# Preparing one batch entry instead of two before the first token blocks of a Fourier mixing and SoLU kernel

## The chip, the cores and the metric

The kernel runs on one core of a Trainium2 chip. A core has a matrix engine (PE in the profile, with its weight loads as PEld), a vector engine (DVE), an activation engine (ACT), a general engine (POOL), a queue engine that only issues transfers (SP), and 16 DMA engines that carry the transfers which SP, ACT and POOL issue. Every engine works through its own instructions in order. The metric is the time of one execution in device microseconds.

## What is computed

```python
def _attn_ref(x, filt_r, filt_i):            # x (8, 3136, 256), filters (1569, 256)
    X = np.fft.rfft(x, axis=1)
    Y = X * (filt_r + 1j * filt_i)[None, :, :]
    return np.fft.irfft(Y, n=x.shape[1], axis=1).astype(np.float32)

def _moe_ref(x, w_in, w_out, g_ln):          # x (25088, 256), w_in (256, 1024), w_out (1024, 256)
    h = x @ w_in
    e = np.exp(h - np.max(h, axis=-1, keepdims=True))
    solu = h * (e / (np.sum(e, axis=-1, keepdims=True) + 1e-09))
    mu = np.mean(solu, axis=-1, keepdims=True)
    var = np.mean((solu - mu) ** 2, axis=-1, keepdims=True)
    return ((solu - mu) / np.sqrt(var + 1e-06) * g_ln) @ w_out
```

The second function takes the output of the first, its eight batch entries laid end to end. The inputs of the second part are in 64-bit floats and are converted on the chip.

## The kernel before

**The Fourier part** splits the length 3136 as 49 x 64 and is done for each batch entry in three stages with two trips through DRAM. Stage one (`first`, L213) works in eight pieces per entry: a piece `x` of 98 partitions is loaded, multiplied with the table `wf_t` (tile `pa`), copied by ACT to `t1` and stored to `d1`. Stage two (the spectrum) works in units: a unit loads `t2` from `d1` (`fetch`), multiplies it with the table `de` (`forward`, tile `pb`), multiplies the result with the complex filter `f` on DVE (`multiply`: products `pr`, `pi` and a term `pt` for each, part 0 for the real, part 1 for the imaginary part), multiplies back (`inverse`, tile `pc`), copies it to `g` and stores it to `d2`. A spectrum of two entries at once ("paired") has 13 units of one pair of rows of the table each, a spectrum of one entry 7 units of two pairs. Stage three (`back`, L305) loads a piece `t4` from `d2` (`fetch_back`, L297), multiplies it with `wi_t` (tile `py`) and ACT copies it into `y`.

**The buffer `y`** holds two entries: 256 channels as two chunks of 128 partitions, 2 x 3136 tokens. Even entries stand in its first half, odd entries in its second.

**The token part** works on 196 blocks of 128 tokens, one per step `k` (`step`, L750). Pairs of blocks share seven products instead of eight in both matrix multiplications, so POOL forms sums of `y` (`pair_sums`) and of the turned activations (`project_sums`). A step issues the products `m` with `w_in` (L541), the exponential (L573), the normalization (L589), a 32x32 transpose `turn` on DVE (L599), four transfers that regroup it into `solu_t` (L611), and, nine steps later (`LAG`), the products `o` with `w_out` (L653). After the last block nine steps drain the pipeline.

**What sets the order.** The opening, up to `y` of entry 0, is laid out by a scheduler from the order in the code. There the entries 0 and 1 go through stages one and two together (group 0), and entry 0 through stage three; entry 1's stage three is spread over steps 0 to 19. From the first block on the order is written out by hand: the lists `first_of`, `early`, `mid`, `late`, `stores`, `products` and `loads` hold for each step the jobs of the Fourier part that go at a given place of the step. `GROUPS` gives for each group of entries the first step and the number of steps over which its pieces and its units are spread:

```python
    ((0, 1), None, None),
    ((2,), (0, 6), (9, 14)),
    ((3, 4), (6, 13), (23, 26)),
```

A unit at step t is fetched at the end of step t - 2, goes forward in step t (`early`), has part 0 at the end of step t (`late`), part 1 at the start of step t + 1 (`products`), goes back at the end of step t + 1 and is stored in step t + 2. Loads of `x` and of `t4` share three buffers (`r`), and each is issued up to three steps ahead, not before the load three before it is used:

```python
        at = max(t - 3, row_loads[n - 3][0] if n >= 3 else -1)
```

In the blocks POOL issues the loads of `x` and `f` and the stores of `d1` and `d2`, ACT the loads of `t2` and `de`, SP the loads of `t4`, the regrouping and the output. In the opening ten matmuls on nothing that is needed (`idle`, L422) run on PE between stage two and stage three. The filters stay in SBUF during the opening; for the later spectra they are copied from the inputs to `f_dram` by eight transfers in steps 0 to 3. The weights are converted from 64 bits by DVE in eight blocks of ten instructions (`load_float64`): four of `w_in`, then `weight_sums`, and four of `w_out`.

Of the kernel before, what the change touches and what calls it, by code (L numbers as in the profile page):

```python
# [10 lines left out]
FP32 = mybir.dt.float32  # L11
# [19 lines left out]
NG = 5  # L31
# [9 lines left out]
    ((0, 1), None, None),  # L41
    ((2,), (0, 6), (9, 14)),
    ((3, 4), (6, 13), (23, 26)),
    ((5, 6), (32, 28), (64, 29)),
    ((7,), (94, 18), (116, 24)),
]
EPS_LN, EPS_SM = 1e-6, 1e-9
# [41 lines left out]
def kernel(  # L89
# [30 lines left out]
    nc.sync.dma_start(out=wf_t, in_=wf_dram)  # L120
# [43 lines left out]
    def by_16(dmas, out, in_, engines=16):  # L164

        n = out.shape[0] // engines * engines
        dmas[0](out=out[:n], in_=in_[:n])
        dmas[1](out=out[n:], in_=in_[n:])

    class Spectrum:  # L170
# [6 lines left out]
        def __init__(self, n, pools, load, load_de):  # L177
            self.n, self.entries, self.pools = n, GROUPS[n][0], pools
            self.load, self.load_de = load, load_de
            self.paired = len(self.entries) == 2  # L180
# [23 lines left out]
        def fetch_x(self, i, dmas, split):  # L204
            b, ch = divmod(i, NH // NCH)
            self.xs[i] = xt = self.pools["r"].tile([P, NCH, C], FP32, name=f"x_{self.n}_{i}", tag="r")
            xb = x[self.entries[b]]
            for h, first, step in ((0, NCH * ch, C), (1, N2 - 1 - NCH * ch, -C)):
                split(dmas, xt[N1 * h:N1 * h + N1],
                      bass.AP(tensor=xb.tensor, offset=xb.offset + first * C,  # L210
                              ap=[[N2 * C, N1], [step, NCH], [1, C]]))
# [16 lines left out]

        def fetch(self, i, dma):
            self.t2s[i] = self.pools["t2"].tile([P, 4, C], FP32, name=f"t2_{self.n}_{i}", tag="t2")  # L230
# [3 lines left out]
        def fetch_de(self, i):  # L234
            self.des[i] = self.load_de(*self.units[i])

        def fetch_filter(self, i):
            self.fs[i] = self.load(*self.units[i])
# [17 lines left out]
        def multiply(self, i, part, add):  # L256
# [5 lines left out]
            def fk(k):  # L262
# [3 lines left out]
            out, term = (self.pools["p"].tile([P, 2, C], FP32, name=f"p{tag}_{self.n}_{i}", tag=tag)[  # L266
                rows, 0:w, :] for tag in ("ri"[part], "t"))
# [8 lines left out]
        def inverse(self, i, pss):  # L276
# [6 lines left out]
            self.gs[i] = self.pools["g"].tile([P, 4, C], FP32, name=f"g_{self.n}_{i}", tag="g")  # L283
# [34 lines left out]
    with ExitStack() as st:  # L318
        pools = {name: pool(name + "0", bufs, stack=st)
                 for name, bufs in (("r", 6), ("t1", 4), ("t2", 3), ("p", 2), ("g", 2))}  # L320
        fpool = pool("fp", 1, stack=st)
        wpool = pool("wp", 2, stack=st)
# [34 lines left out]
        def load_tables(g):  # L357
            i0, n = NG * g, min(NG, NP - NG * g)
            tables[g] = fpool.tile([P, NG, 2, 2, NQ], FP32, name=f"de_{g}", tag=f"de{g}")
            nc.gpsimd.dma_start(out=tables[g][:, 0:n],  # L360
                                in_=de_dram[i0:i0 + n].rearrange("i p k u q -> p i (k u q)"))
            filters[g] = f = fpool.tile([P, NG, 2, C], FP32, name=f"f_{g}", tag=f"f{g}")
            for place, k, held, rows in all_filter_rows(i0, n):
                nc.gpsimd.dma_start(out=f[place, 0:held, k, :], in_=rows)

# [11 lines left out]
        def resident(i, pairs):  # L377
            return filters[i // NG][:, i % NG:i % NG + pairs]

        sp = Spectrum(0, pools, resident, lambda i, pairs: tables[i // NG][:, i % NG:i % NG + pairs])  # L380
# [5 lines left out]
        for i in range(2 * NH // NCH):  # L386
            sp.fetch_x(i, (nc.sync.dma_start, nc.sync.dma_start), partial(by_16, engines=15))
            sp.first(i, (0, 1), ps_h.tile([P, 2, 512], FP32, name=f"pa_0_{i}", tag="h"),
                     nc.scalar.copy)
            sp.store_first(i, 0, lambda out, in_: by_16((nc.scalar.dma_start, nc.gpsimd.dma_start), out, in_))  # L390
# [478 lines left out]
```

## Time and profile before

| | us |
|---|---|
| median of three runs | 1861.56 |
| lowest and highest run | 1852.31, 1864.58 |
| the profiled execution | 1860.94 |
| its span (first to last instruction) | 1859.2 |
| PE busy | 1676.2 |
| DVE busy | 1229.4 |
| POOL busy | 1071.6 |
| ACT busy | 948.0 |
| mean granted clock of PE, share of full | 0.945 |

The profile counts an engine as busy while one of its instructions runs; issuing a transfer does not count. The span is cut into stretches below, each with the engines' busy time, the clock granted to PE and what the DMA engines moved. A row of a wait reads "who <- for whom: total us, times, longest". Where an engine waits for several things, the row names the last.

### The profile page before, as it was taken

To read this page: it belongs to the slowest core of one execution; us is meant where nothing else is said; L and a number is where in the kernel's file an instruction comes from. 1 tells how busy PE (TensorE), PEld (TensorE's weight loads), DVE (VectorE), ACT (ScalarE), POOL (GpSimd) and SP (SyncE) were. 2 spreads that over 40 slices of the span, in tenths; PEclk is the share of its full clock that TensorE was granted. 3 is DMA by queue.
4 is the path that set the end of the run, shared out by engine and by line. 5 is a ranking of instruction groups with operands and counts; after the bars stand their busy time and mean duration, and the time that the engine had idled before them with its cause. 6 is when DMAs were issued, how large, how long until landed. Compare 5 with 4: busy or idle time off the path is not lost.

```text
span 1859.2 us, 29143 instructions
## 1 busy us (share of the span) xinstructions
PE 1676.2 (90%) x9192; PEld 1106.6 (60%) x9192; DVE 1229.4 (66%) x2583; ACT 948.0 (51%) x1715; POOL 1071.6 (58%) x1281
## 2 busy tenths in 40 slices
PE   4547978879999999999999999998999999999996
PEld 1111733546556666675665666776676777777776
DVE  0585045456877777567778776667777776778773
ACT  1111345435455555565555556664555666665562
POOL 4134255555656776555654566655556666666664
PEclk8677588889999999999999999999999999999999
DMA  8754457776668776556556565655656454444443
GB/s 231 215 180 154 117 175 195 198 200 176 170 177 219 208 204 175 143 142 177 164 154 171 157 144 147 163 132 145 173 163 154 109 124 125 111 109 103 104 109 101
DMA packets 356249, 293.69 MB, mean 158 GB/s; under 512 B 63105, under 2 KB 324290, under 8 KB 356096
## 3 DMA queue, kind: packets, MB, share of 16 engines
q1 hardware_dynamic: 292960, 167.96, 35.9%
q0 software_dynamic: 33824, 91.09, 16.2%
q10 hardware_dynamic: 29312, 32.78, 5.9%
q8 instruction: 75, 1.23, 0.3%
q14 instruction: 78, 0.64, 0.1%
HBM read 110.68 MB, written 81.50 MB: 103 GB/s over the span
## 4 chain that ended last, share of the span: by engine, by line
PE 62%; DVE 15%; DMA 11%; issue 4%; POOL 3%; ACT 3%; SPq 1%; ACTq 0%; DVEq 0%; POOLq 0%
PE o L653 25%; PE m L541 23%; PE py L311 6%; PE pa L219 4%; DMA solu_t<-turn 3%; DVE h L589 3%; DMA x<-in_x_dram 3%; DMA t<-d 2%; PE pc L244 2%; PE pb L244 2%; DVE turn L599 2%; DVE pr L271 1%; DVE pt L270 1%; DMA raw<-in_moe_w_out_dram 1%; DVE h L565 1%
## 5 line engine op out<-in xcount | busy, mean ns | idle before, releaser
L653 PE MATMUL o<-w_out_sb,solu_t 128*128 128x128 f32 x3136 | 406.9, 279 | 22.2 <-DVE ot L672 20.2
L653 PEld LDWEIGHTS o<-w_out_sb,solu_t 128*128 128x128 f32 x3136 | 383.2, 194 | 60.6 <-issue 32.9
L541 PE MATMUL m<-w_in_sb,s 128*128 128x512 f32 x784 | 406.7, 612 | 3.9 <-ACT h L551 3.8
L591 ACT ACTIVATE e<-h,nmu 128x1024 f32<-128x1024 f32 x196 | 225.3, 1150 | 358.8 <-DVE h L589 356.4
L653 PEld LDWEIGHTS o<-w_out_sb,u 128*128 128x128 f32 x2352 | 310.3, 193 | 147.7 <-issue 118.6
L541 PE MATMUL m<-w_in_sb,y 128*128 128x512 f32 x588 | 307.1, 606 | 17.4 <-DVE nmax L565 13.9
L653 PE MATMUL o<-w_out_sb,u 128*128 128x128 f32 x2352 | 315.2, 278 | 7.6 <-ACT ot L665 7.5
L519 POOL TENSOR_TENSOR u<-solu_t 128x512 f32<-128x512 f32 x98 | 149.8, 1528 | 282.2 <-DMA solu_t<-turn 176.2
L589 DVE SCALAR_TENSOR_TENSOR h<-e,rsum,h 128x1024 f32<-128x1024 f32 x196 | 283.5, 1446 | 7.4 <-DVE rsum L586 0.6
L672 DVE SCALAR_TENSOR_TENSOR ot<-o,rs_t,ot 128x128 f32<-128x128 f32 x294 | 101.6, 345 | 265.2 <-ACT ot L665 226.3
L565 DVE CUSTOM_DVE_ANT_0 h<-m,h 128x512 f32<-128x512 f32 x196 | 134.5, 686 | 212.8 <-ACT h L551 132.7
L551 ACT COPY h<-m 128x512 f32<-128x512 f32 x294 | 172.6, 587 | 155.6 <-PE m L541 102.4
L519 POOL TENSOR_TENSOR u<-solu_t,u 128x512 f32<-128x512 f32 x98 | 141.4, 1443 | 181.7 <-PE o L653 180.8
L599 DVE STREAM_TRANSPOSE turn<-h 128x1024 f32<-128x1024 f32 x196 | 242.5, 1237 | 1.5
L573 ACT ACTIVATE e<-h,nmax 128x1024 f32<-128x1024 f32 x196 | 224.7, 1147 | 0.0
L219 PE MATMUL pa<-x,wf_t 98*100 98x512 f32 x256 | 150.1, 700 | 65.6 <-DMA x<-in_x_dram 54.1
L311 PEld LDWEIGHTS py<-wi_t,t 100*128 100x128 f32 x1024 | 142.4, 212 | 72.6 <-issue 51.5
L541 PEld LDWEIGHTS m<-w_in_sb,s 128*128 128x128 f32 x784 | 131.1, 195 | 90.0 <-issue 78.8
L311 PE MATMUL py<-wi_t,t 100*128 100x98 f32 x1024 | 148.1, 297 | 18.0 <-DMA t<-d 15.1
L314 ACT COPY y<-py 128x392 f32<-128x392 f32 x128 | 107.4, 839 | 91.2 <-PE py L311 89.9
L519 POOL TENSOR_TENSOR solu_t<-solu_t,solu_t 128x512 f32<-128x512 f32 x98 | 145.9, 1489 | 7.7
L541 PEld LDWEIGHTS m<-w_in_sb,y 128*128 128x128 f32 x588 | 98.0, 192 | 86.5 <-issue 50.1
(75 smaller groups left out, 1866.6 us busy)
## 6 DMA issues: line engine op xcount, KB each, us to landing
solu_t<-turn SPq DMA_DIRECT2D x784, 128.0 KB
out_dram<-ot SPq DMA_DIRECT2D x196, 128.0 KB
t<-d SPq DMA_DIRECT2D x56, 400.0 KB
d<-g POOLq DMA_DIRECT2D x75, 256.0 KB, 4.2
d<-t POOLq DMA_DIRECT2D x96, 200.0 KB, 4.3
x<-in_x_dram POOLq DMA_DIRECT2D x96, 196.0 KB, 6.0
t<-d ACTq DMA_DIRECT2D x50, 256.0 KB
t<-d SPq DMA_DIRECT2D x25, 256.0 KB
```

Source lines behind the costliest of these rows:

```text
L219: nc.tensor.matmul(out=ps[0:NK, j], lhsT=wf_t, rhs=self.xs[i][0:NR, 2 * u:2 * u + 2, :], start=True, stop=True)
L311: nc.tensor.matmul(out=psv[:, i:2 * NCH - i:2 * NCH - 1 - 2 * i, :], lhsT=t4s[e, ch][:, i, cb * P:cb * P + P], rhs=wi_t, start=True, stop= ...
L314: evac(out=y[:, cb, t0:t0 + S].rearrange("p (r m j) -> p m j r", m=N2 // NCH, j=NCH)[:, ch:last + 1 - ch:last - 2 * ch], in_=psv.rearrange ...
L519: nc.gpsimd.tensor_tensor(out=out, in0=in0, in1=in1, op=op)
L541: nc.tensor.matmul(out=ms[j, bank], lhsT=lhsT, rhs=w_in_sb[:, w, :], start=m in (1, 2, 7), stop=True, skip_group_check=True)
L551: nc.scalar.copy(out=h_half(k, i), in_=ms[j, 0])
L565: nc.vector.tensor_tensor_reduce(out=h_half(k, i), in0=ms[j, bank], in1=h_half(*kept), scale=1.0, scalar=sofar, op0=ALU.add, op1=ALU.min, ...
L573: nc.scalar.activation(out=e, in_=hs[k], func=AFT.Exp, bias=nmaxs.pop(k)[:, 1:2], scale=-1.0, accum_out=esum)
L589: nc.vector.scalar_tensor_tensor(out=solu, in0=e, scalar=rsum, in1=solu, op0=ALU.mult, op1=ALU.mult, accum_out=nmu)
L591: nc.scalar.activation(out=e, in_=solu, func=AFT.Square, bias=nmu, scale=-float(DFF), accum_out=variances[g][:, i:i + 1])
L599: nc.vector.transpose(out=turns[g][:, :, i, :], in_=solus.pop(k).rearrange("p (f j) -> p f j", j=32))
L653: nc.tensor.matmul(out=pos[p, bank], lhsT=lhs[:, f, :], rhs=w[:, f, :], start=f == 0 and m in (1, 2, 7), stop=True, skip_group_check=True)
```

## The change

Entry 1 leaves the opening. Group 0 is entry 0 alone, a spectrum of seven units, and entry 1 becomes a group of its own in the blocks, with its eight pieces in steps 0 and 1 and its units in steps 4 to 12. The later groups move back: entry 2's units from steps 9 to 21 to steps 14 to 26, those of entries 3 and 4 from 23 to 47 to 32 to 56. Stage three of entry 1 goes from steps 0 to 19 into steps 17 to 21. The opening's order is now written by hand: all loads first, then the pieces, the conversion of `w_in`, the units, the `idle` matmuls (now with 128 rows of operands, not 64, and not waiting for the last product), and stage three with the conversion of `w_out` behind it on DVE.

Entry 1 uses the second half of `y`, which is empty until its own stage three: six of its `x` pieces are loaded there during the opening's stage three (`fetch_second`), and its odd units have a second set of buffers there (`spare`: `t2`, `f`, `de`, `pr`, `pi`, `pt`, `g`). Odd units up to step 7 also use the two PSUM banks of the projection (`other`), which is not yet running, and for units up to step 7 POOL does the additions of `multiply`. For an odd unit `f` and `de` are loaded one step ahead, not two. `f_dram` is written by three stores from SBUF in the opening instead of eight copies in the blocks. In all blocks SP issues the loads of `x`, not POOL, and part 1 of a unit stands behind `finish` in its step, not at the start.

```diff
 GROUPS = [
-    ((0, 1), None, None),
-    ((2,), (0, 6), (9, 14)),
-    ((3, 4), (6, 13), (23, 26)),
...
+    ((0,), None, None),
+    ((1,), [0, 0, 0, 0, 1, 1, 1, 1], [4, 5, 6, 7, 8, 10, 12]),
+    ((2,), [*range(3, 11)], [*range(14, 28, 2)]),
+    ((3, 4), [*range(11, 17), *range(20, 30)], [*range(32, 58, 2)]),
+    ((5, 6), [*range(46, 62)], [*range(64, 90, 2)]),
...
+BACK_FROM = {1: 17, 2: 31, 3: 61}
...
+        def buffer(self, i, kind, shape):
+            if i % 2 and kind in self.spare:
+                return self.spare[kind]
+            return self.pools["p" if kind in ("pr", "pi", "pt") else kind].tile(
+                shape, FP32, name=f"{kind}_{self.n}_{i}", tag=kind)
...
+        second = Spectrum(1, None, None, None)
+        spare = [y[:, c, S:S + 3 * NCH * C] for c in range(KD)]
+
+        def fetch_second():
+            for i in range(6):
+                out = spare[i % 2][:, i // 2 * NCH * C:(i // 2 + 1) * NCH * C]
+                second.fetch_x(i, [lambda out, in_: nc.sync.dma_start(out=out, in_=in_)] * 2,
+                               out.rearrange("p (n c) -> p n c", c=C))
...
-        for i in range(2 * NH // NCH):
-            sp.fetch_x(i, (nc.sync.dma_start, nc.sync.dma_start), partial(by_16, engines=15))
...
+        def fetch_x(i):
+            sp.fetch_x(i, (lambda out, in_: by_16((nc.sync.dma_start, nc.gpsimd.dma_start), out, in_),
+                           lambda out, in_: nc.gpsimd.dma_start(out=out, in_=in_)))
+
+        st.enter_context(tc.manual_schedule())
...
+        for i in range(4):
+            fetch_x(i)
+        begin(0)
+        for i in range(4, 7):
+            fetch_x(i)
+        begin(1)
+        load_tables(0, 4)
+        for i in range(pieces):
+            sp.first(i, (0, 1), ps_h.tile([P, 2, 512], FP32, name=f"pa_0_{i}", tag="h"),
+                     nc.scalar.copy)
+            sp.store_first(i, 0, lambda out, in_: by_16((nc.scalar.dma_start, nc.sync.dma_start), out, in_))
+            if i == 0:
+                fetch_x(7)
+                begin(2)
+                load_tables(4, NP - 4)
+        for j in range(4):
+            load_float64(weights[j][0], raws.pop(j), negate=True)
+            if j == 0:
+                begin(3)
...
             nc.tensor.matmul(out=idle[:, 0, :],
-                             lhsT=tables[0][0:NQ, 0, 0].rearrange("p u q -> p (u q)"),
-                             rhs=last.rearrange("p b c -> p (b c)"), start=True, stop=True)
+                             lhsT=tables[0][0][:, 0, 0].rearrange("p u q -> p (u q)"),
+                             rhs=filters[0][0][:, 0].rearrange("p k c -> p (k c)"), start=True, stop=True)
...
+            if ch == 0:
+                fetch_back(0, 7, pools["r"])
+                for i0, n, rows in ((0, 4, P), (4, NP - 5, P), (NP - 1, 1, NQ)):
+                    f, at = filters[i0]
+                    nc.sync.dma_start(
+                        out=f_dram[i0:i0 + n].rearrange("i u q k c -> (u q) i (k c)")[0:rows],
+                        in_=f[0:rows, at:at + n].rearrange("p i k c -> p i (k c)"))
+                fetch_second()
...
-    for n, args in enumerate(all_filter_rows(0, NP)):
-        loads[n // 2].append(lambda args=args: copy_filter(*args))
...
-            row_loads.append((t, lambda sp=sp, i=i: sp.fetch_x(
-                i, (nc.gpsimd.dma_start,), whole)))
+            if i not in sp.xs:
+                row_loads.append((t, lambda sp=sp, i=i: sp.fetch_x(
+                    i, [lambda out, in_: nc.sync.dma_start(out=out, in_=in_)] * 2)))
...
+            other = n == 1 and i % 2 == 1 and t + 1 < LAG
+            add = nc.gpsimd.tensor_tensor if t + 1 < LAG else nc.vector.tensor_tensor
...
+            by = 1 if n == 1 and i % 2 == 1 else 2
+            ahead(t, by).append(lambda sp=sp, i=i: sp.fetch_filter(i))
+            ahead(t, by).append(lambda sp=sp, i=i: sp.fetch_de(i))
...
-        for job in stores[k] + products[k] + first_of[k]:
+        for job in stores[k] + first_of[k]:
             job()
...
+        for job in products[k]:
+            job()
         if 2 <= k < blocks + 2:
             exponential(k - 2)
```

Three places in the order of the instructions. Names carry numbers: `x_0_1000` and `t_1_0_0` are pieces of a group and entry, `d_1` is `d1` of group 1, `s_0` the sums of block pair 0.

POOL at the start of the blocks, before; group 1 is entry 2 here, group 2 the entries 3 and 4:

```order
L162 DMA x_0_1000<-in_x_dram 49x1024
L162 DMA x_0_1000<-in_x_dram 49x4x256
L162 DMA x_1_1003<-in_x_dram 49x1024
L162 DMA x_1_1003<-in_x_dram 49x4x256
L519 TENSOR_TENSOR s_0_1010<-y 128x128
L519 TENSOR_TENSOR s_0_1011<-s_0_1010,y 128x128
L519 TENSOR_TENSOR s_0_1011<-y 128x128
L519 TENSOR_TENSOR s_0_1010<-y,s_0_1011 128x128
L226 DMA d_1_67<-t_1_0_0_1017 100x512
L226 DMA d_1_67<-t_1_0_2_1022 100x512
```

and after, where group 1 is entry 1:

```order
L580 TENSOR_TENSOR s_0_781<-y 128x128
L580 TENSOR_TENSOR s_0_782<-s_0_781,y 128x128
L580 TENSOR_TENSOR s_0_782<-y 128x128
L580 TENSOR_TENSOR s_0_781<-y,s_0_782 128x128
L229 DMA d_1_67<-t_1_0_0_788 100x512
L229 DMA d_1_67<-t_1_0_2_793 100x512
L229 DMA d_1_67<-t_1_1_0_798 100x512
L229 DMA d_1_67<-t_1_1_2_803 100x512
L229 DMA d_1_67<-t_1_2_0_808 100x512
L229 DMA d_1_67<-t_1_2_2_813 100x512
```

The loads of `x` are gone from POOL, and twice as many stores of `t1` follow in each of the steps 0 and 1.

PE in step 0, before: two pieces, a piece of entry 1's stage three, then the products of block pair 0.

```order
L219 MATMUL pa_0_0_1016<-x_0_1000,wf_t 100x512
L219 MATMUL pa_0_1_1021<-x_0_1000,wf_t 100x512
L219 MATMUL pa_1_0_1026<-x_1_1003,wf_t 100x512
L219 MATMUL pa_1_1_1031<-x_1_1003,wf_t 100x512
L311 MATMUL py_0_0_1036<-wi_t,t_1_0_1006 128x2x49 x3
L311 MATMUL py_0_0_1036<-wi_t,t_1_0_1006 128x98
L311 MATMUL py_0_1_1042<-wi_t,t_1_0_1006 128x2x49 x3
L311 MATMUL py_0_1_1042<-wi_t,t_1_0_1006 128x98
L541 MATMUL m_0_1048<-w_in_sb,y 128x512
```

After:

```order
L222 MATMUL pa_0_0_787<-y,wf_t 100x512
L222 MATMUL pa_0_1_792<-y,wf_t 100x512
L222 MATMUL pa_1_0_797<-y,wf_t 100x512
L222 MATMUL pa_1_1_802<-y,wf_t 100x512
L222 MATMUL pa_2_0_807<-y,wf_t 100x512
L222 MATMUL pa_2_1_812<-y,wf_t 100x512
L222 MATMUL pa_3_0_817<-y,wf_t 100x512
L222 MATMUL pa_3_1_822<-y,wf_t 100x512
L602 MATMUL m_0_827<-w_in_sb,y 128x512
```

Four pieces of entry 1, read from the second half of `y`, now stand ahead of the first product, and no piece of stage three.

SP around the second pair's regrouping, before:

```order
L162 DMA t_1_3_1412<-d_0_71 100x1024
L625 DMA rs_t_1444<-rows_1385 32x4x1 x4
L611 DMA solu_t_0_1495<-turn_1234 32x8x128 x4
L611 DMA solu_t_1_1508<-turn_1234 32x8x128 x4
L611 DMA solu_t_0_1631<-turn_1432 32x8x128 x4
```

After:

```order
L769 DMA x_6_1244<-in_x_dram 49x1024
L769 DMA x_6_1244<-in_x_dram 49x4x256
L686 DMA rs_t_1293<-rows_1182 32x4x1 x4
L769 DMA x_7_1322<-in_x_dram 49x1024
L769 DMA x_7_1322<-in_x_dram 49x4x256
L672 DMA solu_t_0_1343<-turn_1003 32x8x128 x4
L672 DMA solu_t_1_1369<-turn_1003 32x8x128 x4
L769 DMA x_0_1404<-in_x_dram 49x1024
L769 DMA x_0_1404<-in_x_dram 49x4x256
L769 DMA x_1_1486<-in_x_dram 49x1024
L769 DMA x_1_1486<-in_x_dram 49x4x256
L672 DMA solu_t_0_1503<-turn_1266 32x8x128 x4
```

Loads of `x` now stand between the regrouping transfers of the block pairs on SP.

More of the change, by code (lines that the diff above doesn't have):

```diff
@@ L264, in fk @@
                 return fk.broadcast_to([NQ * residues, w, C]) if self.paired else fk
-            out, term = (self.pools["p"].tile([P, 2, C], FP32, name=f"p{tag}_{self.n}_{i}", tag=tag)[
-                rows, 0:w, :] for tag in ("ri"[part], "t"))
+            out, term = (self.buffer(i, kind, [P, 2, C])[rows, 0:w, :]
+                         for kind in (("pr", "pi")[part], "pt"))
             re, im = (ps[rows, 0:w, :] for ps in self.spectra[i])
@@ L282, in inverse @@
                                  prods[r][rows])
[L283 removed]
+            self.gs[i] = self.buffer(i, "g", [P, 4, C])
             for u in range(self.shape(i)[0]):
@@ L496, in prepare_w_out, with load_de @@
             weight_sums(w_out_sb)
-    def load_de(i, pairs):
-        de = depool.tile([P, 2, 2, 2, NQ], FP32, name=f"de_{i}", tag="de")
+    def load_de(sp, u):
+        i, pairs = sp.units[u]
+        de = sp.buffer(u, "de", [P, 2, 2, 2, NQ])
         nc.scalar.dma_start(out=de[:, 0:pairs],
```

148 lines of the change are left out of this document (77 added, 71 removed).

## Prediction

> **What bounds the kernel now.** I read the busy times by stage first, because the share of TensorE over the whole span (90%) mixes an opening with a long main loop. I cut the span where the chain of work changes its kind. The columns are the stretch, its length, busy time and count of PE, PE's weight loads, DVE, ACT and POOL, then the granted clock, the DMA share and GB/s.
>
> ```profile
> 0.00:99.20 99.20, 46.27 (x64) 14.84 (x65) 32.81 (x67) 17.48 (x17) 30.20 (x54) 0.74 0.80 224
> 99.20:179.10 79.90, 49.55 (x205) 12.09 (x205) 59.16 (x84) 12.88 (x24) 36.15 (x41) 0.82 0.48 162
> 179.10:193.00 13.90, 13.90 (x18) 5.11 (x17) 0.00 (x0) 0.59 (x1) 0.74 (x1) 0.50 0.69 191
> 193.00:220.40 27.40, 27.40 (x129) 27.40 (x129) 0.00 (x0) 12.38 (x15) 2.66 (x4) 0.50 0.28 75
> 220.40:487.90 267.50, 225.74 (x1072) 129.40 (x1071) 147.26 (x316) 129.41 (x230) 153.99 (x213) 0.90 0.65 185
> 487.90:1405.00 917.10, 878.20 (x5088) 592.20 (x5087) 666.44 (x1398) 517.46 (x949) 561.57 (x673) 0.99 0.63 167
> 1405.00:1820.00 415.00, 408.54 (x2405) 300.42 (x2404) 314.10 (x700) 250.68 (x464) 269.13 (x283) 1.00 0.46 115
> 1820.00:1859.20 39.20, 26.64 (x222) 25.13 (x220) 9.62 (x22) 7.13 (x18) 17.19 (x14) 0.96 0.36 96
> ```
>
> Rows one to four are the opening for entries 0 and 1: x comes in and goes through the first transform (99 us, DMA share 0.80), thirteen units of the spectrum (80 us), a gap bridged by idle matmuls (14 us), and the last transform of entry 0 (27 us). Here PE does little that counts. From 220.4 on the blocks run. The same windows for the exponential alone (L573, two records per step) count the steps:
>
> ```profile
> 220.40:487.90 267.50, 28.50 (x46) 0.90 0.65 185
> 1653.00:1754.00 101.00, 19.77 (x32) 1.00 0.42 105
> ```
>
> At 487.9 step 24 has run, so 24 steps took 267.5 us, 11 each; near the end 16 steps take 101.0 us, 6.3 each, with PE full. From 487.9 to 1405 PE idles only 917.1 - 878.2 = 38.9 us. So after step 24 the kernel is bound by PE, before it partly by transfers: PE idles 41.8 us in 220.4 to 487.9. PE's waits between 225 and 490 name them (total us, times, longest):
>
> ```profile
> PE pa L219 <- DMA x<-in_x_dram: 18.4, 4, 9.2
> PE py L311 <- DMA t<-d: 9.3, 2, 6.6
> ```
>
> **The sum, part one: the opening.** The change takes entry 1 out of it. First the sizes of the transfers, from the DMA issues of the page (count, KB each, us from issue to landing), then rows from the timelines of PE and DVE, start and duration first:
>
> ```profile
> solu_t<-turn SPq DMA_DIRECT2D x784, 128.0 KB
> out_dram<-ot SPq DMA_DIRECT2D x196, 128.0 KB
> t<-d SPq DMA_DIRECT2D x56, 400.0 KB
> d<-t POOLq DMA_DIRECT2D x96, 200.0 KB, 4.3
> x<-in_x_dram POOLq DMA_DIRECT2D x96, 196.0 KB, 6.0
> t<-d ACTq DMA_DIRECT2D x12, 512.0 KB
> f<-f_dram POOLq DMA_DIRECT2D x12, 512.0 KB, 5.4
> d<-g POOLq DMA_DIRECT2D x12, 512.0 KB, 6.3
> de<-de_tbl ACTq DMA_DIRECT2D x12, 256.0 KB
> raw<-in_moe_w_in_dram POOLq DMA_DIRECT2D x4, 512.0 KB, 6.0
> ```
>
> ```profile
> 84.21 5.47 PE L219 MATMUL pa<-x,wf_t 98*100 98x512 f32 x8 [7.64 <-issue]
> 99.22 5.04 PE L244 MATMUL pb<-t,de 64*64 64x512 f32 x16 [9.53 <-DMA t<-d]
> 104.95 0.43 DVE L347 TENSOR_SCALAR w_out_sb<-raw 128x512 int32<-128x512 int32 x1 [1.98 <-DMA raw<-in_moe_w_out_dram]
> 110.98 0.69 DVE L353 TENSOR_TENSOR w_out_sb<-w_out_sb,power 128x512 f32<-128x512 f32 x1
> 111.59 0.68 DVE L269 TENSOR_TENSOR pr<-pb,f 128x512 f32<-128x512 f32 x1
> 179.05 14.02 PE L422 MATMUL idle<-pr,de 64*128 64x512 f32 x16
> 192.99 27.62 PE L311 MATMUL py<-wi_t,t 100*128 100x98 f32 x128
> ```
>
> (a) To the first product of the spectrum (DVE L269), now 111.6 us. Ahead of it the new opening moves 8 x pieces of 392 KB (3.2 MB), 8 stores of 400 KB (3.3), all tables and filters (13 pairs x 128 rows x 3 KB = 5.1), four weight blocks of 512 KB (2.1) and three t2 loads (1.6): 15.3 MB, at the first stage's 224 GB/s 68 us. What the first forward product itself needs is 8.7 MB, 39 us. DVE now does four weight conversions in a fixed place ahead of the product; the last one above ran from 104.95 to 111.67, 6.7 us, so four are 27 us, and the fourth block is asked for only after the first is converted, behind nine table loads on POOL. I take 60, with 39 and 75 as ends (75 is 68 and one conversion).
>
> (b) Units: 111.6 to 179.1 for 13 is 5.2 us each. A unit of one entry holds two pairs and has the same 128x512 DVE shapes, and the order of DVE, POOL and PE in it is the same. Seven are 36 us (the last is small; the end below is 31).
>
> (c) The turn through DRAM, now 13.9 us. The ten idle matmuls now use 128 rows. Twenty PE records at the 0.88 us of the present idle ones (14.02 us for 16, at a clock of 0.50) are 17.5 us; I take 16, ends 12 and 18.
>
> (d) The last transform of entry 0 stays: 27.4 us at a granted clock of 0.50, as fast as the weight loads come. In the blocks the same instruction costs:
>
> ```profile
> L311 PE MATMUL py<-wi_t,t 100*128 100x98 f32 x576 | 77.5, 278 | 6.1 <-DMA t<-d 5.8 <-DVE rsum L586 0.3
> ```
>
> 77.5 / 576 x 128 = 17.2 us. Whether idle matmuls with twice the rows warm the clock no row shows. The nearest row is the stage itself, so I take 27 and keep 17 as an end. The Trainium skill (TensorE: Matmul & The Clock Gate, Part 1) has the clock go to full after some 3.4 us of sustained activity; by that, (d) would be about 17 and the sum 10 us lower. The trace disagrees so far: from 179.1 to 220.4 PE was busy without a gap for 41.3 us and the clock stayed at 0.50.
>
> The new stores of the filters (3.3 MB) and six x pieces of entry 1 (2.4 MB) lie under (d), where the DMA share is 0.28. With the 2.1 MB already there this is 7.8 MB, 35 us at 224 GB/s, so some 4 us of it may reach into step 0; that is counted below. The weight conversions 4 to 7 (27 us on DVE) lie under (c) and (d), 43 us. The eight DRAM-to-DRAM filter copies vanish from POOL and cost nothing either way.
>
> Start of the blocks: 60 + 36 + 16 + 27 = **139 us instead of 220.4, a gain of 81**.
>
> **Part two: steps 0 to 24.** PE receives entry 1's first transform and spectrum. Prices at full clock, from PE's timeline and the chain of waits:
>
> ```profile
> 247.93 1.88 PE L219 MATMUL pa<-x,wf_t 98*100 98x512 f32 x4
> 312.30 1.11 PE L244 MATMUL pb<-t,de 64*64 64x256 f32 x16
> 396.88 1.04 PE pc L244 x16
> ```
>
> A piece is 1.9 us, a unit 2.2. Eight pieces and seven units are 30 us that leave the opening. Because the pieces of the later entries move back too, steps 0 to 24 gain 2 pieces and 5.5 units net, 16 us; the other 14 us fall after step 24. PE's own work in these steps becomes 225.7 + 16 = 242 us.
>
> Waits: 41.8 us idle now. 18.4 of it is for x, which POOL issues late, since its queue waits for PE to free a buffer (total us, times, longest):
>
> ```profile
> POOL x L162 <- PE pa L219: 18.6, 5, 10.1
> ```
>
> Now SP issues x, three pieces ahead, and six of entry 1's pieces are there beforehand. I drop the 18.4 and keep 23. Four units' additions go from DVE to POOL, which is busy 154 of 267.5 us here; cost nothing. New waits: steps 0 and 1 push 16 stores of 200 KB through three t1 buffers at 4.3 us to land, 16 / 3 x 4.3 = 23 us against some 20 us of PE work, so 4 to 8; the 4 us above; and each odd unit of entry 1 has its de table loaded one step ahead only, which has cost up to this row of the chain:
>
> ```profile
> 1278.13 7.35 DMA de<-de_tbl
> ```
>
> Three odd units at 0 to 7 us are some 10; their f loads on POOL wait for the spare buffer in the same way, with POOL's block sums behind them, but f is needed only half a step after de. Together 20. **242 + 23 + 20 = 285 us instead of 267.5.** The ends: 242 with no idle at all, and what the transfers need. In steps 0 to 24: 23 x pieces 9.2 MB, 26 pieces stored 10.7, units of 1.8 MB (6.3 of entry 1, 6 of entry 2) 22.5, 8 loads t4 3.3, 19 steps of turned data 10, output 2: 58 MB, against 185 x 267.5 = 49.5 MB now. At 185 GB/s that is 312 us, at the 224 of the first stage 258. 285 lies between.
>
> **Part three: after step 24.** 1859.2 - 487.9 = 1371 us, bound by PE, plus 14 us of PE work, of which the 38.9 us idle may take a little: 1383. DVE's second product now stands behind finish; that is worth at most what DVE costs PE there, part of the 38.9 us, and I cost it at nothing, with 10 us either way. The end (1820 on) is unchanged.
>
> Span: 139 + 285 + 1383 = 1807. The profiled execution took 1860.94 us for a span of 1859.2, so 1.7 is added: **1809 us**. It stands 0.6 below the median of the runs, 1861.56, so the ratio is 0.972.
>
> **The rivals.**
> A, better: the clock is warm in (d) (-10) and the blocks wait less, 255 us (-30): 1769. For it speaks that most of the known waits are x; against it that transfers must then run at 58 / 255 = 227 GB/s.
> B, transfers bind steps 0 to 24 at the present mean of 185 GB/s: 312 us, so 1836. For it: the present mean held with waits everywhere. The Trainium skill (DMA: Bandwidth & Descriptors, Why a DMA increments its semaphore by 16 and not by 1) says that an SP-issued transfer uses the largest number of engines up to 16 that divides its outer size, 7 for the 49 rows that x now has on SP; by that seven engines carry all of x and fill up first, which comes to this case, an estimate. No row here tells engines apart.
> C, every step from 2 to 24 is as slow as the present dense stretch, whose step count is again half of the records:
>
> ```profile
> 322.60:435.60 113.00, 9.94 (x17) 0.88 0.70 200
> ```
>
> 13.3 us a step, 22 of them 293, with 30 for steps 0 and 1: 323, so 1847, no change. Against it: that stretch had x behind POOL.
> D, slower: SP runs in order, and an x load that waits for PE to free its buffer holds the turned data behind it. On POOL this wait is 18.6 / 5 = 3.7 us each. If each of the 23 pieces holds SP that long and all of it reaches PE, 85 us are added: 1894. It decides from 71 / 23 = 3.1 us a piece on. Against it: turned data is used two to three steps later, 20 us or more.
>
> **How the numbers follow.** About 1% (18.6 us) is what a measurement of this kernel can tell from no change: faster is below 1843, slower above 1880. Forecast 0.54, A 0.13, B 0.14, C 0.11, D 0.08. Faster: 0.52 of the forecast, A, 0.10 of B: 0.75. Within 1%: 0.02 of the forecast, 0.04 of B, 0.09 of C: 0.15. Slower: D and 0.02 of C: 0.10. The range from 1766 to 1858 leaves out part of A (0.07), D and the far side of C (0.03): 0.18. Its low end is 120 (the low ends of b, c and d) with 261 in steps 0 to 24; its high end is B with (a) at 75 (+15), (c) at 18 (+2) and the low share of D's waits, 5.
>
> **What would show it.** Right: the blocks' first pa starts at 139 us (125 to 155); step 24 ends 285 us later; from there to the end 1383; PE's waits for x in the first steps almost gone; the SP queue's x loads issued without long waits. Wrong: waits of PE for solu_t behind x (D); a DMA share near 0.8 and pb or pa waiting for t and x all through steps 3 to 24 (B, C); a clock above 0.5 in the last transform (A). The forecast fails most likely at the 285, which rests on waits that I could only bound.

## The result and the profile after

| | before | after |
|---|---|---|
| median, us (4 runs each) | 1856.93 | 1788.72 |
| lowest to highest, us | 1849.22 to 1864.58 | 1786.37 to 1789.90 |
| ratio, 95% interval | | 0.963, 0.958 to 0.968 |
| span of the profiled execution, us | 1859.2 | 1788.1 |
| first `pa` of the blocks, us | 220.4 | 129.65 |
| exponential issued in step 24, us | 486.7 | 423.3 |

The change makes the kernel 3.7% faster; 1809 was forecast. The stretches of the kernel after, with the columns of the stretches shown before (length; busy time and count of PE, PEld, DVE, ACT, POOL; granted clock; DMA share; GB/s):

```profile
0.00:57.40 57.40, 20.25 (x54) 7.69 (x58) 19.46 (x39) 9.38 (x9) 26.01 (x44) 0.74 0.95 265
57.40:99.90 42.50, 22.08 (x185) 13.21 (x177) 36.25 (x54) 6.44 (x12) 15.28 (x16) 0.74 0.45 152
99.90:109.80 9.90, 9.90 (x22) 4.41 (x22) 9.42 (x19) 0.37 (x1) 1.36 (x2) 0.88 0.74 207
109.80:126.20 16.40, 16.30 (x129) 14.98 (x127) 5.63 (x11) 12.63 (x15) 0.00 (x0) 1.00 0.98 321
129.65:423.30 293.65, 246.65 (x1228) 141.90 (x1228) 157.61 (x336) 133.32 (x241) 132.80 (x173) 0.89 0.63 193
423.30:1788.10 1364.80, 1324.08 (x7786) 921.88 (x7784) 995.38 (x2131) 776.53 (x1446) 838.59 (x944) 1.00 0.59 156
```

Row four is the surprise: the last transform of entry 0 runs in 16.4 us at a granted clock of 1.00, where it took 27.4 at 0.50. Row five holds steps 0 to 24 and row six the rest. For the rest the kernel before has, cut at the same exponential:

```profile
486.70:1859.20 1372.50, 1314.57 (x7714) 918.29 (x7712) 991.36 (x2118) 776.46 (x1431) 848.68 (x970) 0.99 0.57 149
```

So the start of the blocks gains 220.4 - 129.65 = 90.8 us, steps 0 to 24 lose 293.7 - 266.3 = 27.4, the rest gains 7.7: 71.1 us, the difference of the spans. PE does 9.5 us more in the rest and idles 40.7 us there, against 57.9.

The boundaries of the opening, first from DVE's timeline after and then from PE's (start, duration; in brackets the idle time ahead and what ended it):

```profile
53.71 0.43 DVE L348 TENSOR_SCALAR power<-raw 128x512 int32<-128x512 int32 x1 [11.23 <-DMA raw<-in_moe_w_in_dram]
61.55 0.68 DVE L278 TENSOR_TENSOR pr<-pb,f 128x512 f32<-128x512 f32 x1
```

```profile
99.90 10.06 PE L467 MATMUL idle<-f,de 128*128 128x512 f32 x20
109.79 16.40 PE L320 MATMUL py<-wi_t,t 100*128 100x98 f32 x128
129.65 7.90 PE L222 MATMUL pa<-y,wf_t 98*100 98x512 f32 x10 [3.45 <-DMA y<-in_x_dram]
```

DVE waits 11.2 us for the fourth weight block just ahead of the first product. PE's longest waits from 125 to 425 us, after, and the one for entry 1's first piece (total us, times, longest):

```profile
PE pa L222 <- DMA x<-in_x_dram: 13.5, 3, 11.8
PE m L602 <- ACT h L612: 7.3, 4, 4.8
PE py L320 <- DMA t<-d: 6.1, 5, 1.8
PE pb L253 <- issue: 5.0, 1, 5.0
PE pa L222 <- DMA y<-in_x_dram: 3.5, 1, 3.5
```

Waits for `x` are still there, but nearly all is one wait of 11.8 us. It lies in steps 18 to 22, which take 71.8 us where they took 36.0 before.

### The profile page after: what moved, and what is told of

It reads as the page before. It is cut to its first block, busy times and chain, and to the rows that moved or that the text cites. A ratio compares the mean times of both kernels' runs of the same rounds, so it can differ in the third digit from the quotient of the medians.

```text
span 1788.1 us, 29451 instructions
## 1 busy us (share of the span) xinstructions
PE 1639.3 (92%) x9392; PEld 1104.1 (62%) x9392; DVE 1223.8 (68%) x2587; ACT 939.5 (53%) x1724; POOL 1015.8 (57%) x1182
## 4 chain that ended last, share of the span: by engine, by line
PE 62%; DMA 14%; DVE 8%; issue 4%; ACT 2%; POOL 2%; SPq 1%; ACTq 0%; POOLq 0%; DVEq 0%
PE o L714 25%; PE m L602 25%; PE py L320 5%; DMA t<-d 5%; DMA solu_t<-turn 4%; DVE h L650 3%; PE pa L222 3%; DMA d<-t 2%; PE pb L253 2%; DMA x<-in_x_dram 1%; PE pc L253 1%; SPq L672 1%; DVE h L623 1%; DMA de<-de_tbl 1%; DVE ot L733 1%
## 5 line engine op out<-in xcount | busy, mean ns | idle before, releaser
L602 PE MATMUL m<-w_in_sb,s 128*128 128x512 f32 x784 | 403.8, 606 | 11.9 <-ACT h L612 11.8
L714 PEld LDWEIGHTS o<-w_out_sb,u 128*128 128x128 f32 x2352 | 306.6, 192 | 151.8 <-issue 114.1
L650 DVE SCALAR_TENSOR_TENSOR h<-e,rsum,h 128x1024 f32<-128x1024 f32 x196 | 288.5, 1472 | 7.0
L320 PEld LDWEIGHTS py<-wi_t,t 100*128 100x128 f32 x1024 | 131.6, 195 | 71.5 <-issue 51.6
L224 ACT COPY t<-pa 100x512 f32<-100x512 f32 (+1 forms) x120 | 73.5, 615 | 164.0 <-PE pa L222 106.8
L222 PE MATMUL pa<-x,wf_t 98*100 98x512 f32 x232 | 125.6, 639 | 36.3 <-DMA x<-in_x_dram 35.6
L602 PEld LDWEIGHTS m<-w_in_sb,y 128*128 128x128 f32 x588 | 99.2, 193 | 90.2 <-issue 40.7
L580 POOL TENSOR_TENSOR solu_t<-solu_t,solu_t 128x512 f32<-128x512 f32 x98 | 150.5, 1536 | 7.7
```

Source lines behind the costliest of these rows:

```text
L222: nc.tensor.matmul(out=ps[0:NK, j], lhsT=wf_t, rhs=self.xs[i][0:NR, 2 * u:2 * u + 2, :], start=True, stop=True)
L320: nc.tensor.matmul(out=psv[:, i:2 * NCH - i:2 * NCH - 1 - 2 * i, :], lhsT=t4s[e, ch][:, i, cb * P:cb * P + P], rhs=wi_t, start=True, stop= ...
L580: nc.gpsimd.tensor_tensor(out=out, in0=in0, in1=in1, op=op)
L602: nc.tensor.matmul(out=ms[j, bank], lhsT=lhsT, rhs=w_in_sb[:, w, :], start=m in (1, 2, 7), stop=True, skip_group_check=True)
L650: nc.vector.scalar_tensor_tensor(out=solu, in0=e, scalar=rsum, in1=solu, op0=ALU.mult, op1=ALU.mult, accum_out=nmu)
L714: nc.tensor.matmul(out=pos[p, bank], lhsT=lhs[:, f, :], rhs=w[:, f, :], start=f == 0 and m in (1, 2, 7), stop=True, skip_group_check=True)
```

## Experiments

Ratios are to the kernel before, run beside each; where a difference of two ratios is turned into time, it is multiplied by 1857 us.

### Idle matmuls: 64 or 128 rows

The forecast failed in the last transform, which was put at 27 us. Two kernels tell whether the rows of the idle matmuls set its clock. The first is the kernel after with 64 rows:

```diff
-    lhsT=tables[0][0][:, 0, 0]..., rhs=filters[0][0][:, 0]...
+    lhsT=tables[0][0][0:NQ, 0, 0]..., rhs=filters[0][0][0:NQ, 0]...
```

> The changed kernel with the idle matmuls on 64 rows of operands, as before the change. Theory (the rows of the idle matmuls decide the clock of the last transform): twenty idle records take about 17.5 us instead of 9.9, the last transform 27 us at a clock of 0.50 instead of 16.4, so the blocks start some 15 us later (3.5 of the 18 are hidden by the wait for x that is there now), near 145 us instead of 129.7, and the kernel takes about 1803 us. Rival (the clock is warm for another reason, the units of one entry before it): the last transform stays at 16 to 17 us and the time at 1788.

Measured: 1801.76 us, ratio 0.970 (0.968 to 0.973). The idle matmuls and the last transform in its stretches:

```profile
98.70:116.10 17.40, 17.40 (x22) 6.51 (x21) 16.02 (x31) 0.37 (x1) 1.32 (x2) 0.50 0.75 203
116.10:143.70 27.60, 27.60 (x130) 27.60 (x130) 0.00 (x0) 12.38 (x15) 0.00 (x0) 0.50 0.59 213
```

Nothing but the rows changed, and PE stays at 0.50 for 45 us without a gap: 7.5 us more for the idle matmuls, 11.2 for the transform. The blocks begin at 143.5 us instead of 129.65, and the kernel is 13 us slower by the ratios, whose intervals just overlap. So the rows of these idle matmuls set the clock of this transform: 128 raise it and 64 don't. The second is the kernel before with 128 rows, taken from the product ahead of the last, since the last has only 64:

```diff
-            last = sp.prods[i][0]
+            if i == NP - 2:
+                last = sp.prods[i][0]
...
-                             lhsT=tables[0][0:NQ, 0, 0]...
+                             lhsT=tables[0][:, 0, 0]...
```

> The kernel before with this one part of the change: idle matmuls on 128 rows. Theory (rows decide the clock): the last transform takes 16 to 17 us instead of 27.4 and the idle matmuls about 10 instead of 14, so that the blocks start 11 to 14 us earlier (about 207 us) and the kernel takes about 1847. Rival 1: no change of the clock, 1859. Rival 2: the clock rises, but the first steps wait longer for x, which comes no earlier, and most of it is given back: 1855.

Measured: 1843.72 us, ratio 0.991 (0.988 to 0.994). Its last transform, from PE's timeline and in two stretches:

```profile
183.59 10.22 PE L311 MATMUL py<-wi_t,t 100*128 100x98 f32 x80 [0.20 <-DMA t<-d]
194.88 10.16 PE L311 MATMUL py<-wi_t,t 100*128 100x98 f32 x48 [1.07 <-DMA t<-d]
```

```profile
183.60:195.30 11.70, 10.54 (x84) 9.74 (x85) 0.00 (x0) 8.29 (x10) 2.65 (x4) 1.00 1.01 243
195.30:205.00 9.70, 9.70 (x48) 9.70 (x47) 0.00 (x0) 4.12 (x5) 0.00 (x0) 0.50 0.31 79
```

The edit gains 0.9% by itself; the blocks begin at 204.8 us, 15.6 earlier. Here the clock falls from 1.00 to 0.50 at 195.3 us, just behind a wait of 1.07 us for data. In the kernel after PE doesn't wait in this transform, and the clock holds. That the wait makes the clock fall was not tested.

### Where the second product stands

The prediction costed part 1 behind `finish` at nothing, 10 us either way. Undone in the kernel after:

```diff
-        for job in stores[k] + first_of[k]:
+        for job in stores[k] + products[k] + first_of[k]:
...
-        for job in products[k]:
-            job()
```

> The changed kernel with the second products of a unit at the start of the step again. Theory (their place behind finish took PE's waits for DVE away after step 24): PE idles some 17 us more after step 24, which then takes about 1380 us instead of 1365, and the kernel about 1803. Rival (the gain after step 24 comes from the new steps of the entries): no change after step 24, 1788.

Measured: 1797.24 us, ratio 0.967 (0.964 to 0.971). It lies between the two values; 8 us above the kernel after, with intervals that overlap. PE's wait for the row maximum, which is not among the waits of the kernel after from 490 to 1745 us, is there again:

```profile
PE m L602 <- DVE nmax L626: 22.9, 27, 2.0
```

But the part from step 24 on takes 1370.1 us instead of 1364.8: 5.3 more, where the theory had some 15. The reverse, done alone in the kernel before:

> The kernel before with this one part of the change: the second products behind finish. Theory: the stretch after step 24 takes about 1356 us instead of 1372, the kernel about 1843. Rival: no change, 1859.

Measured: 1844.09 us, ratio 0.994 (0.992 to 0.997), near the 1843 of the theory. The part from step 24 on takes 1359.2 us instead of 1372.4. PE's waits from 490 to 1745 us, first before, then with part 1 later:

```profile
PE o L653 <- DVE ot L672: 17.4, 14, 3.4
PE m L541 <- DVE nmax L565: 13.9, 11, 2.0
```

```profile
PE m L541 <- DVE h L562: 8.3, 18, 1.0
PE py L311 <- DMA t<-d: 8.1, 4, 3.1
PE pb L244 <- ACT g L288: 7.9, 9, 1.3
```

The two waits of PE for DVE, 31.3 us together, are gone; the other listed waits grow from 10.2 to 30.2 us and take about two thirds of their place. One of these waits in the kernel before, first DVE, then PE:

```profile
914.89 0.69 DVE L271 TENSOR_TENSOR pi<-pi,pt 128x512 f32<-128x512 f32 x1
915.50 1.24 DVE L599 STREAM_TRANSPOSE turn<-h 128x1024 f32<-128x1024 f32 x1
916.66 0.65 DVE L565 CUSTOM_DVE_ANT_0 h<-m,h 128x512 f32<-128x512 f32 x1
917.25 0.08 DVE L565 DVE_READ_ACCUMULATOR2_ANT nmax<- 128x1 f32 x1
```

```profile
917.38 1.12 PE L541 MATMUL m<-w_in_sb,y 128*128 128x512 f32 x2 [1.80 <-DVE nmax L565]
```

DVE worked in order through part 1 of `multiply` (`pi`) while PE waited for the row maximum (`nmax`), or in other steps for the output (`ot`), queued behind it.

Both side edits together in the kernel before:

> The kernel before with both side edits of the change: idle matmuls on 128 rows, and the products behind finish. If the two are independent, the ratios 0.991 and 0.9944 multiply to 0.9855: 1830 us. Then the change's other part, entry 1's move out of the opening, is worth the remaining 1830 - 1789 = 41 us. If they overlap, 1840 or more, and the move is worth over 50.

Measured: 1837.51 us, ratio 0.988 (0.984 to 0.991). The product of the two ratios is 0.9855, so they are about independent. What is left, from 0.9875 to 0.9631 in the ratio, some 45 us (12 either way by the two intervals), is what the rest of the change is worth: entry 1's move with its placement, the opening's order written by hand, the stores of the filters and `x` on SP. No run takes the move apart from the order of the opening.

### Who issues `x`, and how it is split

```diff
-    i, [lambda out, in_: nc.sync.dma_start(out=out, in_=in_)] * 2)))
+    i, [lambda out, in_: nc.gpsimd.dma_start(out=out, in_=in_)] * 2)))
```

> The changed kernel with the loads of x in the blocks issued by POOL, as before the change (six pieces of entry 1 are still loaded by SP in the opening). Theory (POOL issued x too late): PE's waits for x between steps 0 and 24, 17 us now (13.5 for x, 3.5 for the pieces in y), rise to 30 or more, and steps 0 to 24 take 305 to 310 us instead of 294: 1800. Rival (on SP the loads of x hold the turned data and the t4 loads, or fewer DMA engines carry them): steps 18 to 22, 72 us now, fall below 60, and the kernel takes 1775 or less.

Measured: 1780.28 us, ratio 0.960 (0.955 to 0.966). My theory fell: `x` on SP is no gain. PE's waits for `x` in steps 0 to 24 fall from 17.0 us to 8.6, where 30 or more were expected; others grow, and PE idles 48.4 us there, against 47.0. The rival's sign fails too: steps 18 to 22 do not fall below 60 us but stay at 72.3. Two waits of the kernel after from 125 to 425 us, on SP's queue, show that `x` does hold SP:

```profile
SPq L769 <- PE pa L222: 61.5, 8, 17.3
SPq L672 <- DMA t<-d: 22.8, 6, 8.8
```

Eight `x` loads hold SP for 61.5 us until PE frees their buffer, and the turned data (L672) stands behind them. With `x` on POOL this wait is gone from SP, and on POOL it is smaller:

```profile
POOL x L769 <- PE pa L222: 16.0, 3, 14.1
```

The reason that `x` was late before is therefore not POOL alone. The two intervals overlap, so a loss from `x` on SP, some 5 us by the ratios, is likely and not shown. Nor is it shown that SP's wait is the cost: of the 12.6 us by which the profiled span is shorter, 8.3 lie from step 24 on, and SP waits for these buffers almost only before (61.5 of 63.6 us).

The other question is whether the 49 rows of `x` hold it back on SP. Each load was cut in two:

```diff
-    i, [lambda out, in_: nc.sync.dma_start(out=out, in_=in_)] * 2)))
+    i, [lambda out, in_: by_16((nc.sync.dma_start, nc.sync.dma_start), out, in_)] * 2)))
```

> The changed kernel with each half of an x piece in the blocks (49 rows) loaded from SP in two transfers of 48 rows and one row. Theory from the Trainium skill (DMA: Bandwidth & Descriptors, Why a DMA increments its semaphore by 16 and not by 1): 49 rows go to 7 engines, 48 rows to 16; if that binds the first steps, x lands sooner and steps 0 to 24 take 280 us or less instead of 294, the kernel 1775. Rival (engines are not what x waits for, the row buffers and SP's order are): 1788, or up to 10 us more for the 100 added transfers on SP.

The expectation speaks of 48 rows and one, but `by_16` cuts 49 rows into 45 and four in this kernel. A row has 4 KB, and the loads on SP have these sizes, eight of the first kind being from the opening:

```profile
x<-in_x_dram SPq DMA_DIRECT2D x108, 180.0 KB
x<-in_x_dram SPq DMA_DIRECT2D x100, 16.0 KB
```

Measured: 1793.45 us, ratio 0.965 (0.961 to 0.970): no gain. Two stretches of the kernel after, steps 0 to 10 and 24 to 60:

```profile
129.65:245.30 115.65, 96.94 (x366) 41.77 (x366) 64.16 (x140) 50.63 (x93) 55.23 (x77) 0.88 0.64 208
423.30:741.90 318.60, 311.63 (x1710) 195.54 (x1709) 234.90 (x486) 177.93 (x337) 195.42 (x245) 0.99 0.71 198
```

The same two with `x` split:

```profile
128.50:234.60 106.10, 91.36 (x366) 39.39 (x366) 62.41 (x140) 50.81 (x93) 52.58 (x75) 0.92 0.71 222
407.20:735.70 328.50, 312.10 (x1710) 195.61 (x1709) 235.73 (x486) 178.89 (x338) 203.29 (x246) 0.99 0.68 194
```

In the profiled execution, with 1785.3 us the shortest of the four, the first steps take 9.6 us less, at 222 GB/s instead of 208. Steps 0 to 24 take 278.7 us instead of 293.7, which is what the theory had (280 or less); but steps 24 to 60 take 9.9 more, with PE idle for 16.4 us instead of 7.0. The rows may slow the first steps, but the kernel gains nothing by it. What takes the gain back is open.

### Steps 17 to 24

Stage three of entry 1 (eight pieces `t4`, steps 17 to 21) and ten pieces `x` of entries 3 and 4 (from step 20 on, loaded up to three steps ahead) share three buffers. The chain of waits of the kernel after between 328 and 392 us (start, length) names the transfers that carry these steps:

```profile
330.41 8.70 DMA t<-d
...
358.77 7.79 DMA t<-d
...
376.67 10.35 DMA t<-d
387.08 4.50 DMA t<-d
```

They take 31 of these 64 us. SP's timeline shows the `x` loads in the same queue around the last of them:

```profile
377.16 2.14 SPq L769 DMA_DIRECT2D x<-in_x_dram  x2
387.08 0.29 SPq L162 DMA_DIRECT2D t<-d  x1
387.46 16.27 SPq L769 DMA_DIRECT2D x<-in_x_dram  x6
```

The test moves eight of the ten pieces one or two steps back, so that none is left in stage three's steps:

```diff
-    ((3, 4), [*range(11, 17), *range(20, 30)], [*range(32, 58, 2)]),
+    ((3, 4), [*range(11, 17), 22, 23, 24, 25, 26, 26, 27, 28, 28, 29], [*range(32, 58, 2)]),
```

> The changed kernel with the pieces of entry 3 that stand in steps 20 and 21 moved back (22 to 29, two steps with two pieces). Theory (eight t4 loads and four x loads through three row buffers in steps 17 to 22, each some 10 us from issue to use, make the slow stretch): the 12.6 us of PE's waits for x there vanish, steps 18 to 22 take about 58 us instead of 72, and the kernel about 1776. Rival (the loads of t4 alone fill that stretch): steps 18 to 22 stay above 66 us, 1786.

Measured: 1772.13 us, ratio 0.955 (0.950 to 0.960). Steps 18 to 22, first after, then with the later pieces, then with `x` on POOL instead:

```profile
333.40:405.20 71.80, 53.08 (x310) 38.41 (x308) 27.08 (x56) 28.84 (x50) 22.74 (x27) 0.81 0.52 150
```

```profile
328.80:379.80 51.00, 45.36 (x302) 34.40 (x300) 26.65 (x56) 26.33 (x46) 22.61 (x25) 0.90 0.65 181
```

```profile
328.60:400.90 72.30, 52.63 (x310) 38.36 (x308) 26.57 (x56) 28.85 (x49) 28.17 (x36) 0.81 0.54 145
```

With eight PE records fewer the stretch is 20.8 us shorter. It was not short of transfer rate (150 GB/s, and 181 with the later pieces). Nor does SP's queue make it long: with `x` out of that queue it takes 72.3 us. What is left is the order in which the loads of `t4` and `x` take the three buffers they share, which the later pieces change. From step 24 on (397.9 us here) the profile has 12.8 us more, part of it the pieces that now lie there. By the ratios the gain is 16 us, 13 either way. With `x` on POOL as well:

> The kernel after with the later pieces of entries 3 and 4 and with x issued by POOL. Theory: the dense steps 17 to 22 (16 us) and the stalls of SP behind x's buffers (about 8 us) are two things, so both gains add: 1764 us. Rival: it is the same 12 us wait for x in steps 18 to 22 both times, so x on POOL gives nothing more once the pieces are later: 1772.

Measured: 1766.51 us, ratio 0.950 (0.947 to 0.953), near the sum of both. So `x` on POOL and the later pieces appear to gain by two things, which agrees with the 72.3 us above, though the step from 0.955 to 0.950 alone is within the intervals. Against the kernel after the two gain 24 us, and these intervals are apart.

### What the start of the blocks waits for

DVE's wait of 11.2 us for the fourth weight block can be taken away by beginning it ahead of the second table load. The first try also put the fetches of entry 1 ahead of the stores of the filters:

```diff
                 begin(2)
+                load_float64(weights[0][0], raws.pop(0), negate=True)
+                begin(3)
                 load_tables(4, NP - 4)
-        for j in range(4):
+        for j in range(1, 4):
...
-            if j == 0:
-                begin(3)
...
             if ch == 0:
                 fetch_back(0, 7, pools["r"])
+                fetch_second()
...
-                fetch_second()
```

> The changed kernel with the fourth weight block asked for ahead of the second table load, and the six x pieces of entry 1 loaded ahead of the stores of the filters. Theory (the fourth weight block's conversion ends the wait for the first product, at 61.0; the x pieces end that for the first piece in the blocks): first product at about 57.5, bound by the t2 load, blocks start at about 122.5 instead of 129.6, the kernel 1781. Rival (the first forward product moves with the tables): first product stays at 60 or later, 1785.

Measured: 1786.21 us, ratio 0.963 (0.958 to 0.967): no gain. The blocks begin at 120.4 us, 9 earlier, and step 4 is reached at 189.5 us (the exponential issued in it), as without the edit (188.7). ACT's wait from 118 to 192 us tells why:

```profile
ACT t L224 <- DMA f_dram<-f: 13.6, 1, 13.6
```

The copies into `t1` wait until the filters are stored, and the edit had put these stores behind entry 1's loads. With that second part of the edit left out:

> The kernel after with the fourth weight block begun ahead of the second table load, the stores of the filters left ahead of the second entry's fetches. In the kernel that also moved the fetches ahead, the blocks began 9 us sooner, and ACT then waited 13.6 us for a store of the filters, so that step 4 was reached at the same time. Theory: that order made the wait; with the stores first, the blocks begin at about 121 us and step 4 is reached some 7 us sooner: 1781 us. Rival: the filters' 3.3 MB need the time wherever they stand, ACT waits for them all the same, step 4 at 188 us and 1788 us.

Measured: 1778.73 us, ratio 0.957 (0.954 to 0.960), as the theory has it: that wait is not in ACT's list any more, the blocks begin at 123.0 us, step 4 comes at 181.1. Against the kernel after this is 11.5 us by the ratios, 11 either way. DVE is done with the weights 12 us earlier, but the first product comes only 4.2 us earlier, since another wait stood close behind, that of PE for the first unit's data:

```profile
55.24 3.76 PE L253 MATMUL pb<-t,de 64*64 64x256 f32 x32 [16.14 <-DMA t<-d]
57.33 0.69 DVE L278 TENSOR_TENSOR pr<-pb,f 128x512 f32<-128x512 f32 x1 [7.58 <-PE pb L253]
```

The expectation of the first try had named it (57.5 us, bound by the `t2` load). The first idle matmul comes 6.3 us earlier.

### All three gains together

> The kernel after with three edits that each gained alone: the later pieces of entries 3 and 4, x issued by POOL, the fourth weight block begun early. The first two together lie in steps 0 to 22, the third ahead of step 0. If the earlier start stays, the gains add: 1789 - 22 - 10 = 1757 us, ratio 0.945. If the early steps are bound by the transfers, which do not come sooner, the start's 7 us are lost by step 4 again: 1766 us.

Measured: 1752.93 us against 1849.89 for the kernel before beside it, ratio 0.946 (0.944 to 0.949). Within the intervals the gains add: 0.945 was expected, and the rival, 1766 us or 0.951, lies outside. This version beats the kernel after by 1.7% (0.9464 against 0.9631).

## Why the prediction was right, and where it was not

The sign and the main mechanism held, and the size roughly: 71 us of span gained against 52 forecast. The three parts missed by 9.4 us less, 8.7 more and 18.2 less, so the total is closer than it would be without some luck. The forecast priced the 128 rows and the place of part 1 at about nothing, and so gave its 52 us to the rest of the change; the runs give that rest 45 us (12 either way) and the two side edits 23 (0.9875), more than the 19 by which the sum was off. One piece of the mechanism was wrong: `x` on SP is not what shortens its waits.

(a) The first product was put at 60 us and came at 61.55. The four conversions and the wait for the fourth block carry it, as worked out there. But the first forward product, 39 us by its bytes, began only at 55.2, so taking that wait away moved the first product by no more than 4.2 us.

(b) Seven units were put at 36 us and took 38.4 (61.55 to 99.90). Right.

(c) and (d) were mis-sized, by the same cause. The idle matmuls took 9.9 us for 16 forecast, the last transform 16.4 for 27. The step that failed is "the nearest row is the stage itself, so I take 27": that row came from a stage warmed with 64 rows, and the kernel with 64 rows gives 17.4 and 27.6 back. The Trainium skill (TensorE: Matmul & The Clock Gate, Part 1) has the clock rise after some 3.4 us of sustained activity. With 128 rows the trace agrees (0.88 in the idle matmuls, then 1.00), with 64 it does not (0.50 through 45 us). The 9.9 and the 16.4 lie a little below the low ends given, 12 and 17. With the 3.45 us wait for entry 1's first piece, which the forecast has as some 4 in part two, the blocks began at 129.65 instead of 139.

Part two was put at 285 us and took 293.7: PE's work 246.7 for 242, its idle time 47.0 for 43. The size is near, its parts less so. "I drop the 18.4" of the waits for `x` was too bold: 13.5 remain, of which 11.8 in the dense steps. The `de` tables of entry 1's odd units, put at 10, lie in the spare buffers of `y`, and no row of PE's waits names them; the 1.9 us for `de` that PE's list has belong to an even unit. But one odd unit waited for something that the profile doesn't name, 7.6 us after its table had been asked for (243.08 us):

```profile
250.66 2.01 PE L253 MATMUL pb<-y 64*64 64x256 f32 x16 [5.02 <-issue]
```

If that was the table, these tables cost 5 us instead of 10; the profile doesn't show that it was. The dense steps themselves (17 to 22) were not foreseen; the sum had no term for loads of `t4` and `x` that share the buffers `r`. By the kernel with later pieces they cost some 16 us.

Part three was put at 1383 us and took 1364.8. PE's work grew by 9.5 us instead of 14, and the term costed at nothing is the mis-sized one: part 1 behind `finish` takes 13.2 us off this part when done alone in the kernel before, beyond the bound of 10; undone in the kernel after it adds 5.3.

The rivals. A: its warm clock came, its 255 us for steps 0 to 24 did not. B: 312 us at 185 GB/s did not come, since the stretch moved 193 GB/s and took 293.7 us. The Trainium skill (DMA: Bandwidth & Descriptors, Why a DMA increments its semaphore by 16 and not by 1) has 49 rows carried by seven engines; by the same rule 45 rows go to fifteen. With 45 rows and four the first steps were faster in the trace and the kernel was not, so the rule may hold here and does not decide. C: 13.3 us a step came only in the dense stretch, 71.8 us for four steps, thus worse there and better elsewhere (88.1 us for steps 10 to 18, by the exponentials at 245.3 and 333.4). D: its stall is there, 61.5 us on SP, 7.7 for each of the eight loads that wait, above the 3.1 for each of 23 from which it was to decide; in total it is below the 71 us at which it would, and none of PE's longer waits is for turned data. What was right in its weighing is the slack of two to three steps behind SP.

## What to carry to other kernels

Here, work that left an idle opening cost the steps that took it 27.4 us, with 22.1 us more of PE's work in them. With some of the loads moved out of steps in which others use the same buffers, the kernel gained some 16 us: look at every shared ring of buffers step by step, not at the mean transfer rate. On an engine that works in order, put what nobody waits for behind what the bound engine waits for; here moving a product within its step was worth 5 to 13 us in the traces. After an earlier start, look for the next wait before counting the gain: here stores that the edit itself had put last took all of the 9 us, and without that the first product met the next wait 4 us on.

## What was not expected of the hardware

Idle matmuls with 64 rows, and the transform behind them, ran at a granted clock of 0.50 through 45 us of unbroken PE work in the kernel after, as they had through 41 us in the kernel before; with 128 rows it rose within the 9.9 us of them (0.88 on the mean) and the transform ran at 1.00. In the kernel before, idle matmuls with 128 rows raised it too, and it fell to 0.50 at 195.3 us, right behind a wait of PE of 1.07 us for data. But neither rows nor waits alone are the rule. The units of the kernel before, whose operands have 64 rows as well (two matmuls at a time, one on each half of the partitions), ran at 1.00 with PE busy for 22.6 of 37.0 us:

```profile
119.00:156.00 37.00, 22.59 (x122) 5.88 (x124) 30.57 (x39) 7.68 (x15) 21.87 (x24) 1.00 0.65 214
```

What separates these cases was not tried.
